# The attention front of a retention layer with two MLPs: fewer chunks ahead of the decay table, compact states, and output rests made by TensorE

## The chip, the cores and the metric

The kernel runs on one core of one Trainium2 chip. The metric is device microseconds of one execution. A core has TensorE (PE: matrix products out of SBUF into PSUM; PEld is its weight load), VectorE (DVE), ScalarE (ACT), GpSimd (POOL) and SyncE (SP). SP and ScalarE also issue DMA transfers, each on a queue of its own; 16 DMA engines carry them. Each engine works through its instructions in program order and waits on semaphores for the others.

## The reference

A retention (linear attention) layer comes first, with a decay factor `lam` for each of 8 heads, over 2 batches of 768 tokens, head size 64. Its output, 1536 tokens of 512 channels, goes through two MLPs (512 to 2048 to 512). The first has a leaky rectifier with a learned slope, the second a squared rectifier.

```python
for b in range(nb):
    intra = np.einsum('bhic,bhjc->bhij', qb, kb) * Dmask[None]     # lam ** (i - j), lower triangle
    intra = np.einsum('bhij,bhjd->bhid', intra, vb)
    inter = np.einsum('bhid,bhde->bhie', qb * lam_pow[None], kv_state)
    out[:, :, sl] = intra + inter
    kb_dec = kb * rev_pow[None]
    kv_state = lam_block[None, :, None, None] * kv_state + np.einsum('bhsd,bhse->bhde', kb_dec, vb)
...
h = x @ w_in
g = np.maximum(h, 0.0) + alpha * np.minimum(h, 0.0)     # second MLP: g = np.maximum(h, 0.0) ** 2
return (g @ w_out).astype(np.float32)
```

The weights are float64, and everything else is float32.

## The kernel before

**Precision.** A product of the MLPs is three passes over float32r operands (12 bits of mantissa): each operand is split into a float32r value `h` and the exact rest `l`, and lh, hl and hh are summed in PSUM. So whatever enters an MLP is needed twice: `xh` (a cast) and `xl = x - xh`. The attention runs in plain float32, which TensorE does in two passes per product.

**Weights.** They arrive as raw float64 bits in 64 pieces of 512 KB. Piece 2f is the f-th slice (128 hidden channels) of the first w_in, piece 2f + 1 that of w_out; pieces from 32 on are the second MLP's. `load_piece` issues a piece on ScalarE's queue, three ahead. `Conversion` turns a piece into float32r and rest: `start` (two ScalarE operations, issued one piece ahead), `begin` (three VectorE operations), `middle` (one VectorE operation, then ScalarE's cast `wh`, then the load of a further piece) and `end` (VectorE: `wl`). One such round is called a unit below. Before, pieces are converted in the order 0, 1, 2, ...

**The decay table.** VectorE computes powers of `lam` on 8 partitions into `z`, SP writes `z` to HBM (`zd`) and reads it back in two skewed forms, `dec` (the mask, 128 x 8 x 128) and `grow` (powers for the state's part). The ten loads of q and k for five chunks are issued ahead of `zd` on SP's queue, and v, r (the keys again, tokens on partitions) of chunks 0 and 1 on ScalarE's.

**Attention.** There are 12 chunks of 128 tokens: chunk index 0 to 5 with the two batches alternating, so chunk n + 2 continues chunk n's state. The eight heads go in four pairs. For each chunk:

- `scores(n)`: k^T q, eight products on two row tiles (64 x 128) into two PSUM banks. Chunks 0 to 4 (LA = 5) run ahead of the table; ScalarE copies their scores to SBUF.
- `decay(n)`: VectorE multiplies the scores by `dec`, in two halves, from SBUF for chunks 0 to 4 and out of PSUM for the others.
- `factors(n)`: GpSimd multiplies q by `grow` and r by a column of `dec`.
- `outputs(n)`: TensorE adds into one bank `po`: v and decayed scores (two column tiles), then the state times q (full 128 x 128, the state being a block diagonal of two heads with zeros beside it). `pk` is r^T v, again a full 128 x 128 product of which only the two diagonal blocks are used.
- `keep_output(n)`: ScalarE casts `po` to `xh`, VectorE subtracts for `xl`.
- `keep_state(n)`: VectorE adds the two diagonal blocks of `pk` to the decayed old state, one instruction for each; ScalarE scales the new state by lam ** 128 in four instructions, for the chunk after next.

The loop over n writes the order of each engine out by hand: loads for later chunks, `outputs(n)`, `decay(n + 4)`, a unit if `EARLY_UNITS[n]` says so (chunks 3 to 8 and 10: seven units), `keep_output(n)`, `keep_state(n)`, `factors(n + 2)`, `scores(n + 5)`. The decays of a unit chunk stand between the steps of `begin`.

**MLPs.** Then come 48 steps per MLP, each for one tile of 512 tokens and one hidden slice: `first` (12 passes into one of three banks), activation, `rest`, and, two steps later, `second` (12 passes into four of five banks). The first six steps are slices 0 to 5 of token tile 0, so each needs two new pieces of weights; one piece is converted per step.

PSUM has eight banks; before, one pool holds tags for them, and attention and MLPs take turns on them.

Of the kernel before, what the change touches and what calls it, by code (L numbers as in the profile page):

```python
# [23 lines left out]
TT = 512  # tokens of an MLP tile  # L24
# [17 lines left out]
def retention_then_two_mlps(  # L42
# [26 lines left out]
    psum = ctx.enter_context(tc.tile_pool(name="psum", bufs=1, space=PSUM))  # L69
# [4 lines left out]
    used = {}  # L74

    def bank(name, banks):
        """The next of some banks of PSUM."""
        i = used[banks] = used.get(banks, -1) + 1
        return psum.tile([128, 512], F32, tag=f"bank{banks[i % len(banks)]}", name=name)

    def pair_bank(name, banks):
        return bank(name, banks).rearrange("p (a i) -> p a i", a=NPAIR)

# [6 lines left out]
    # Piece 2 f is the slice of w_in for the f-th 128 hidden channels, piece 2 f + 1 that of w_out.  # L90
    # Piece j of 4 NF: the second pair's come behind the first's.
    wpools = {}
    raws, bits, weights = {}, {}, {}

    def load_piece(j):
        if j < 4 * NF:
            raws[j] = raw = rawp.tile([128, DM, 2], U32, tag="raw", name=f"raw{j}")
            w = (w1, w2)[j // (2 * NF)]
            nc.scalar.dma_start(raw.rearrange("p a b -> p (a b)"), w[j % (2 * NF)])

    class Conversion:
        def __init__(self):
            self.j = 0

        def start(self, j):
            if j < 4 * NF:
# [5 lines left out]
        def begin(self, between=()):  # L112
            """Exponent of 11 -> 8 bits: its top bit and its low 7. Below float32's range all are 0."""
            between = iter(between)
            if self.j == 0:
                self.start(0)
            self.start(self.j + 1)
            x, high = bits[self.j], raws[self.j][:, :, 1]
            nc.vector.tensor_scalar(x.bitcast(F32), x.bitcast(F32), LEAST, None, ALU.max)  # L119
            next(between, lambda: None)()  # L120
            nc.vector.tensor_scalar(x, x, 3, 0x3FFFFFF8, ALU.logical_shift_left, ALU.bitwise_and)  # L121
            next(between, lambda: None)()
# [4 lines left out]
        def middle(self):  # L127
            """The lower word, rounded to the last three bits."""
            j = self.j
# [4 lines left out]
            load_piece(j + AHEAD)  # L134
            weights[j] = hi

        def end(self):
            j = self.j
# [4 lines left out]
            self.j += 1  # L143
# [6 lines left out]
    # (MLP, token tile, hidden slice, slices that are summed in PSUM together)  # L150
# [64 lines left out]
    def partial_sum(m, t, f, part, i):  # L215
# [3 lines left out]
        # The same operand stays in the array where it can.  # L219
# [52 lines left out]
    z = ap1.tile([H, ZW], F32, name="z")  # L272
    nc.vector.memset(z[:, 0 : CH - 1], 0.0)
    qk_t, vk_t = {}, {}
# [8 lines left out]
    def load_vk(n):  # L283
        queue = nc.scalar if n < 2 else nc.sync
        v_t = kp.tile([128, H, D], F32, tag="v", name=f"v{n}")
        queue.dma_start(v_t, vr[n])
        r_t = None
        if ORDER[n][0] < NCH - 1:
            r_t = kp.tile([128, H, D], F32, tag="r", name=f"r{n}")
            queue.dma_start(r_t, kr[n])  # L290
# [5 lines left out]
    pw = pair_bank("warm_ps", (0, 2))  # L296
    for i in range(WARM):
        nc.tensor.matmul(pw[:, i % NPAIR, :], warm, warm, start=True, stop=True)

# [292 lines left out]
```

## Time and profile before

| | |
|---|---|
| time, median of 3 runs | 602.98 us (602.83 to 604.35) |
| span of the profiled execution | 600.4 us (the page lists no other time of this execution) |
| TensorE busy | 578.9 us, 96% |
| VectorE busy | 360.7 us, 60% |
| ScalarE busy | 298.0 us, 50% |
| GpSimd busy | 29.8 us, 5% |
| first product of the MLPs starts | 74.43 us into the span |
| DMA moved | 54.23 MB |

Busy shares are means over the span. The attention and the MLPs load the engines in quite different ways, so they are read stage by stage. The profile's times count from the first instruction of the span. `xN` behind a row is the number of instructions in it. On TensorE a float32 product counts as two matmul instructions, and the ends of matmuls are modelled, so distances between starts tell more than durations.

### The profile page before, as it was taken

The numbers are of one execution on the slowest core, as the hardware profiler recorded it, in microseconds if no ns is written. First come the engines' busy times: TensorE is split into PE (matmuls) and PEld (weight loads), VectorE is DVE, ScalarE is ACT, GpSimd is POOL, SyncE is SP. The second block draws the span as 40 slices with busy tenths as digits, with TensorE's granted clock in tenths as the row PEclk, the third lists the DMA queues.
The fourth block names the chain that finished last, engine by engine and source line by source line (L and its number), as shares of the span: only waits on it lengthen the run. The fifth ranks groups of instructions, "written<-read, shape, count | busy, mean of one in ns | idle before, by whom it ended". The sixth has DMA issues, their size and how long they took to land.

```text
span 600.4 us, 7487 instructions
## 1 busy us (share of the span) xinstructions
PE 578.9 (96%) x2868; PEld 481.8 (80%) x2868; DVE 360.7 (60%) x625; ACT 298.0 (50%) x515; POOL 29.8 (5%) x29
## 2 busy tenths in 40 slices
PE   7697699999999999999999999999999999999997
PEld 6586588888888888888888888888888888888886
DVE  3889989675777777777887797773222222222221
ACT  4254678665666676665676465542322222322222
POOL 1674000000000000000000000000000000000000
PEclk9698999999999999999999999999999999999999
DMA  8994333324422231233333232210100000100001
GB/s 285 345 301 140 106 106 128 131 94 158 157 90 88 105 106 62 79 105 106 105 109 102 72 105 96 81 36 0 72 0 1 0 1 1 70 1 0 1 1 70
DMA packets 21667, 54.23 MB, mean 90 GB/s; under 512 B 2424, under 2 KB 3968, under 8 KB 21632
## 3 DMA queue, kind: packets, MB, share of 16 engines
q10 hardware_dynamic: 9792, 34.61, 16.6%
q1 hardware_dynamic: 11840, 19.16, 9.4%
q8 instruction: 22, 0.36, 0.2%
q14 instruction: 13, 0.11, 0.1%
HBM read 48.50 MB, written 5.25 MB: 90 GB/s over the span
## 4 chain that ended last, share of the span: by engine, by line
PE 89%; DVE 6%; DMA 2%; issue 1%; ACT 1%; DVEq 0%; SPq 0%
PE h L167 43%; PE acc L225 22%; PE acc L223 22%; DMA dec<-zd 1%; DVE sc L392 1%; DVE state L449 1%; PE o L417 1%; DVE bits L131 1%; DVE wl L141 1%; DVE bits L119 1%; DVE xal L441 1%; DMA zd<-z 1%; PE pk L431 1%; DVE bits L123 0%; DVE bits L121 0%
## 5 line engine op out<-in xcount | busy, mean ns | idle before, releaser
L177 DVE SCALAR_TENSOR_TENSOR g<-h,g 128x512 f32<-128x512 f32 x48 | 33.1, 691 | 127.9 <-ACT g L176 127.9
L186 ACT CAST gh<-g 128x512 fp32r<-128x512 f32 x96 | 59.6, 621 | 85.8 <-DVE g L177 37.8
L176 ACT ACTIVATE g<-h 128x512 f32<-128x512 f32 x48 | 28.7, 597 | 133.2 <-PE h L167 133.2
L191 DVE TENSOR_TENSOR gl<-g,gh 128x512 fp32r<-128x512 f32 x96 | 66.5, 692 | 32.0 <-ACT gh L186 24.9
L167 PE MATMUL h<-xah,wl 128*128 128x512 f32 x192 | 74.8, 390 | 0.0
L167 PE MATMUL h<-xah,wh 128*128 128x512 f32 x192 | 74.7, 389 | 0.0
L223 PE MATMUL acc<-gh,wh 128*128 128x512 f32 x192 | 74.7, 389 | 0.0
L225 PE MATMUL acc<-wh,gh 128*128 128x512 f32 x192 | 74.7, 389 | 0.0
L167 PE MATMUL h<-xal,wh 128*128 128x512 f32 x192 | 74.7, 389 | 0.0
L223 PE MATMUL acc<-gl,wh 128*128 128x512 f32 x192 | 74.7, 389 | 0.0
L167 PE MATMUL h<-xbh,wl 128*128 128x512 f32 x192 | 74.7, 389 | 0.0
L225 PE MATMUL acc<-wh,gl 128*128 128x512 f32 x192 | 74.7, 389 | 0.0
L223 PE MATMUL acc<-gh,wl 128*128 128x512 f32 x192 | 74.7, 389 | 0.0
L167 PE MATMUL h<-xbl,wh 128*128 128x512 f32 x192 | 74.7, 389 | 0.0
L167 PE MATMUL h<-xbh,wh 128*128 128x512 f32 x192 | 74.7, 389 | 0.0
L225 PE MATMUL acc<-wl,gh 128*128 128x512 f32 x192 | 74.7, 389 | 0.0
L181 DVE SCALAR_TENSOR_TENSOR g<-h,g 128x512 f32<-128x512 f32 x44 | 30.4, 691 | 44.1 <-ACT g L180 44.0
L133 ACT CAST wh<-bits 128x512 fp32r<-128x512 f32 x64 | 39.8, 622 | 17.3 <-DVE bits L131 17.2
L123 DVE SCALAR_TENSOR_TENSOR bits<-raw,bits 128x512 uint32<-128x512 uint32 x64 | 44.2, 691 | 2.0
L141 DVE TENSOR_TENSOR wl<-bits,wh 128x512 fp32r<-128x512 f32 x64 | 44.5, 695 | 0.9 <-ACT wh L133 0.7
L131 DVE CUSTOM_DVE_ANT_0 bits<-raw,bits 128x1024 uint16<-128x1024 uint16 x64 | 44.7, 698 | 0.0
L109 ACT ACTIVATE bits<-raw 128x512 f32<-128x512 f32 x64 | 42.9, 671 | 0.0
(74 smaller groups left out, 833.0 us busy)
## 6 DMA issues: line engine op xcount, KB each, us to landing
raw<-in_w_dram ACTq DMA_DIRECT2D x64, 512.0 KB, 3.3
k<-in_kt_dram SPq DMA_DIRECT2D x12, 256.0 KB, 5.4
q<-in_qt_dram SPq DMA_DIRECT2D x12, 256.0 KB, 5.6
out_dram<-p SPq DMA_DIRECT2D x12, 256.0 KB, 2.3
v<-in_vr_dram SPq DMA_DIRECT2D x10, 256.0 KB, 4.9
r<-in_kr_dram SPq DMA_DIRECT2D x8, 256.0 KB, 5.2
sums<-p SPq DMA_DIRECT2D x8, 256.0 KB, 2.2
ps<-sums SPq DMA_DIRECT2D x8, 256.0 KB, 3.0
```

The costliest lines, as they stand in the source:

```text
L109: nc.scalar.activation(x.bitcast(F32), high.bitcast(F32), AF.Abs)
L123: nc.vector.scalar_tensor_tensor(x, high, 0xC0000000, x, ALU.bitwise_and, ALU.bitwise_or)
L131: nc.vector.tensor_tensor(x.bitcast(I32), x.bitcast(I32), low.bitcast(I32), ALU.add)
L133: nc.scalar.copy(hi, x.bitcast(F32))
L141: nc.vector.tensor_tensor(lo, x, hi.bitcast(F32), ALU.subtract)
L167: nc.tensor.matmul(ph, w[:, cols], x[:, c, :], start=c == 0 and i == 0, stop=c == NC - 1 and i == 2)
L177: nc.vector.scalar_tensor_tensor(g, ph, 0.0, g, ALU.max, ALU.mult)
L181: nc.vector.scalar_tensor_tensor(g, ph, 0.0, g, ALU.max, ALU.subtract)
L186: nc.scalar.copy(gh, g)
L191: nc.vector.tensor_tensor(gl, g, gh.bitcast(F32), ALU.subtract)
L223: nc.tensor.matmul(acc[t][i], w[:, cols], g, **flags)
L225: nc.tensor.matmul(acc[t][i], g[:, cols], w, **flags)
```

## The change

- Three chunks (LA = 3) run their scores ahead of the decay table instead of five, and the pools of q, k, v, r keep their number of buffers (scores have four instead of six). Raw piece 0 is loaded at the very front (ScalarE's queue) and v, r of chunk 0 stand on SP's queue between `zd` and `dec`; those of chunk 1 and q, k of chunk 3 follow `grow`.
- The tensor engine's warming products are 12 ahead of the scores and 10 behind those of chunk 2.
- Piece 0 is converted before the loop, and five more in the loop (chunks 3, 5, 6, 8, 9): six in all. Pieces are converted and loaded in the order 0, 2, 1, 4, 3, 6, 5, ... The loads of the early pieces go on SP's queue.
- Scores of a chunk are one PSUM tile of two banks; a decay is one instruction of 128 x 1024, out of SBUF for chunks 0 and 1 and out of PSUM from chunk 2 on. It is issued two chunks ahead (DA).
- A state holds only its two 64 x 64 blocks (128 x 4 x 64). Its product with q is eight products of 64 x 64, and `pk` eight of 128 x 64. VectorE's add is one instruction of 128 x 256.
- `xl` is no longer made by VectorE: TensorE adds -I times `xh` to `po` (float32r, one product of 512 columns), after the scores of a later chunk, and ScalarE copies the result to `xl`.
- Attention has PSUM pools of its own (two buffers for scores, outputs and pk each), and the MLPs' pool is opened behind them.

```diff
-LA = 5  # chunks whose scores run ahead
+LA = 3
+DA = 2
-WARM = 10  # products that only warm the tensor engine up
-EARLY_UNITS = [0, 0, 0, 1, 1, 1, 1, 1, 1, 0, 1, 0]  # whether a weight piece goes with a chunk
+WARM = 12, 10
+EARLY_UNITS = [0, 0, 0, 1, 0, 1, 1, 0, 1, 1, 0, 0]
+SEQ = [0] + [p for f in range(1, 2 * NF) for p in (2 * f, 2 * f - 1)] + [4 * NF - 1]
...
-    def load_piece(j):
-        if j < 4 * NF:
+    def load_piece(queue=nc.scalar):
+        if len(loaded) < 4 * NF:
+            j = SEQ[len(loaded)]
+            loaded.append(j)
...
-            nc.scalar.dma_start(raw.rearrange("p a b -> p (a b)"), w[j % (2 * NF)])
+            queue.dma_start(raw.rearrange("p a b -> p (a b)"), w[j % (2 * NF)])
...
-            load_piece(j + AHEAD)
+            if load:
+                load_piece(nc.sync if len(loaded) < 2 * EARLY else nc.scalar)
...
-    qp = actx.enter_context(tc.tile_pool(name="qp", bufs=LA + 2))
-    kp = actx.enter_context(tc.tile_pool(name="kp", bufs=LA))
+    qp = actx.enter_context(tc.tile_pool(name="qp", bufs=LA + 4))
+    kp = actx.enter_context(tc.tile_pool(name="kp", bufs=LA + 2))
...
+    psc = actx.enter_context(tc.tile_pool(name="psc", bufs=2, space=PSUM))
+    pso = actx.enter_context(tc.tile_pool(name="pso", bufs=2, space=PSUM))
+    psk = actx.enter_context(tc.tile_pool(name="psk", bufs=2, space=PSUM))
...
+    def keep_warm(i):
+        pw = pso.tile([128, NPAIR, CH], F32, tag="o", name=f"warm_ps{i}")
+        for a in range(WARM[i]):
+            nc.tensor.matmul(pw[:, a % NPAIR, :], warm, warm, start=True, stop=True)
+    less = ap1.tile([128, CH], F32R, name="less")
+    lessf = ap1.tile([128, CH], F32, name="lessf")
+    nc.gpsimd.affine_select(
+        lessf, warm, pattern=[[-1, CH]], compare_op=ALU.not_equal, fill=-1.0, base=0,
+        channel_multiplier=1,
+    )
+    nc.scalar.copy(less, lessf)
+    keep_warm(0)
+    load_piece()
     for n in range(LA):
         load_qk(n)
...
     nc.sync.dma_start(zd, z)
+    load_vk(0)
...
+    load_vk(1)
+    load_qk(LA)
...
-            st = ap1.tile([128, NPAIR, 128], F32, name=f"state{b}_{r}")
-            nc.gpsimd.memset(st, 0.0)
-            state[b, r] = st
+            state[b, r] = ap1.tile([128, NPAIR, D], F32, name=f"state{b}_{r}")
...
-        if n < LA:
-            for t in range(2):
-                nc.scalar.copy(sc[:, t], ps[t])
-            sc_t[n] = sc, None
-        else:
-            sc_t[n] = sc, ps
+        if n < LA - 1:
+            nc.scalar.copy(sc, ps)
+            ps = sc
+        sc_t[n] = sc, ps
...
-        nc.vector.tensor_tensor(sc[:, t], s, dec_v[:, t], ALU.mult)
+        nc.vector.tensor_tensor(sc, ps, dec_v, ALU.mult)
...
-                nc.tensor.matmul(
-                    po[:, a, :], state[b, c % 2][:, a, :], q_t[:, a, :], start=False, stop=True,
-                    skip_group_check=True,
-                )
+                for t in range(2):
+                    d = slice(t * D, (t + 1) * D)
+                    nc.tensor.matmul(
+                        po[d, a, :], state[b, c % 2][d, a, :], q_t[d, a, :], start=False,
+                        stop=True, skip_group_check=True,
+                    )
...
-                nc.tensor.matmul(
-                    pk[:, a, :], r_t[:, 2 * a : 2 * a + 2, :], v_t[:, 2 * a : 2 * a + 2, :],
-                    start=True, stop=True,
-                )
+                for t in range(2):
+                    h = 2 * a + t
+                    nc.tensor.matmul(
+                        pk[t * D : (t + 1) * D, a, :], r_t[:, h, :], v_t[:, h, :], start=a == 0,
+                        stop=True, skip_group_check=True,
+                    )
...
         nc.scalar.copy(xh[:, :, cols], po)
-        nc.vector.tensor_tensor(xl[:, :, cols], po, xh.bitcast(F32)[:, :, cols], ALU.subtract)
+    def keep_rest(n, po):
...
+        nc.tensor.matmul(po, less, xh[:, :, cols], start=False, stop=True, skip_group_check=True)
+        nc.scalar.copy(xl[:, :, cols], po)
...
     for n in range(LA):
         scores(n)
         if n == 0:
-            load_vk(0)
-            load_vk(1)
+            conv.start(0)
+    keep_warm(1)
+    conv.begin(ahead=False)
+    conv.middle(load=False)
+    conv.end()
     for n in range(2):
         factors(n)
-    for n in range(LA):
-        for t in range(2):
-            decay(n, t)
+    for n in range(DA):
+        decay(n)
     for n in range(NN):
         if n + 2 < NN:
             load_vk(n + 2)
-        for i in [LA, LA + 1] if n == 0 else [n + LA + 1]:
-            if i < NN:
-                load_qk(i)
+        if n + LA + 1 < NN:
+            load_qk(n + LA + 1)
+        if n in (1, 2, 3):
+            load_piece(nc.sync)
...
         po, pk = outputs(n)
-        late = []
-        if LA <= n + LA - 1 < NN and n > 0:
-            late = [lambda t=t: decay(n + LA - 1, t) for t in range(2)]
+        if n + DA < NN:
+            decay(n + DA)
         if EARLY_UNITS[n]:
-            conv.begin(late)
+            conv.begin()
...
         keep_output(n, po)
-        if EARLY_UNITS[n]:
-            conv.middle()
         if pk is not None:
             keep_state(n, pk)
         if EARLY_UNITS[n]:
+            conv.middle()
             conv.end()
         if n + 2 < NN:
             factors(n + 2)
         if n + LA < NN:
             scores(n + LA)
+        keep_rest(n, po)
     actx.close()
+    psum["mlp"] = ctx.enter_context(
+        tc.tile_pool(name="psum", bufs=1, space=PSUM, reuse_waits="tile")
+    )
```

## Rows read from the trace of the kernel before

**Rows 1.** Busy time of each engine by stretch: us, then busy (instructions) for each.

```profile
29.64:46.34 16.70, 16.66 (x195) 14.93 (x193) 14.52 (x25) 9.24 (x22) 12.18 (x11) 1.00 0.92 309
46.34:74.43 28.09, 19.72 (x193) 17.00 (x193) 26.86 (x48) 16.73 (x37) 6.63 (x5) 0.94 0.33 113
74.43:597.00 522.57, 522.52 (x2307) 432.48 (x2305) 302.49 (x506) 260.91 (x435) 0.00 (x0) 1.00 0.20 69
...
61.30:66.60 5.30, 3.14 (x35) 2.73 (x34) 5.22 (x11) 3.52 (x9) 0.00 (x0) 1.00 0.31 109
```

**Rows 2.** Chain of waits in order of time: start, us, what.

```profile
0.74 1.33 DMA lam_sb<-in_lam_dram
...
7.68 3.61 DMA zd<-z
11.35 6.43 DMA dec<-zd
17.88 3.05 DVE sc L392 x2
...
588.79 8.17 PE acc L225 x36
```

**Rows 3.** Timeline of TensorE, chunk 0 and chunk 2: start, us, group.

```profile
20.98 1.97 PE L417 MATMUL o<-sc,v 128*64 128x128 f32 x14 [0.78 <-DVE sc L392]
...
29.64 1.09 PE L417 MATMUL o<-sc,v 128*64 128x128 f32 x16
30.67 1.16 PE L423 MATMUL o<-q,state 128*128 128x128 f32 x8
31.66 1.06 PE L431 MATMUL pk<-v,r 128*128 128x128 f32 x8
32.65 1.16 PE L378 MATMUL s<-q,k 64*128 64x128 f32 x16
```

**Rows 4.** Waits of TensorE, 17.88 to 74.43: total, times, longest.

```profile
PE o L417 <- DVE xal L441: 4.6, 4, 1.8
```

**Rows 5.** DMA rate in the first 20 us, slices of 0.5 us.

```profile
GB/s 0 0 0 0 33 299 397 307 217 234 291 361 381 397 344 356 389 401 389 397 404 404 393 393 391 225 345 293 280 240 269 202 252 202 237 282 331 356 377 402
```

**Rows 6.** Groups by shape, first 75 us: count, busy us, mean ns, idle before.

```profile
L392 DVE TENSOR_TENSOR sc<-sc,dec 128x512 f32<-128x512 f32 x10 | 10.9, 1155 | 10.2 <-DMA dec<-zd 10.2
...
L392 DVE TENSOR_TENSOR sc<-s,dec 128x512 f32<-128x512 f32 x14 | 9.4, 682 | 0.2
...
L440 ACT CAST xah<-o 128x512 fp32r<-128x512 f32 x11 | 6.3, 572 | 10.4 <-PE o L417 9.3 <-PE o L423 1.1
```

**Rows 7.** The same for VectorE, 56 to 67 us.

```profile
L449 DVE TENSOR_TENSOR state<-pk,old 64x256 f32<-64x256 f32 x4 | 1.7, 418 | 0.0
L441 DVE TENSOR_TENSOR xal<-o,xah 128x512 fp32r<-128x512 f32 x2 | 1.4, 680 | 0.0
L123 DVE SCALAR_TENSOR_TENSOR bits<-raw,bits 128x512 uint32<-128x512 uint32 x2 | 1.4, 679 | 0.0
...
L119 DVE TENSOR_SCALAR bits<-bits 128x512 f32<-128x512 f32 x3 | 1.3, 418 | 0.0
```

**Rows 8.** The same for VectorE, 38 to 45 us.

```profile
L119 DVE TENSOR_SCALAR bits<-bits 128x512 f32<-128x512 f32 x1 | 1.3, 1276 | 0.0
```

**Rows 9.** Stretches, TensorE alone: us, busy, granted clock, DMA share, GB/s.

```profile
13.20:14.00 0.80, 0.01 (x1) 1.00 1.14 325
...
15.50:16.00 0.50, 0.00 (x0) 0.65 1.12 202
...
25.50:26.00 0.50, 0.50 (x8) 0.61 1.07 324
```

**Rows 10.** Timeline of VectorE, steps 2 and 3 of the MLPs.

```profile
90.53 0.69 DVE L141 TENSOR_TENSOR wl<-bits,wh 128x512 fp32r<-128x512 f32 x1
...
94.90 0.68 DVE L141 TENSOR_TENSOR wl<-bits,wh 128x512 fp32r<-128x512 f32 x1
```

**Rows 11.** Timeline of TensorE, first product of step 5.

```profile
96.31 0.39 PE L167 MATMUL h<-xah,wl 128*128 128x512 f32 x1
```

More of the change, by code (lines that the diff above doesn't have):

```diff
@@ L74, in retention_then_two_mlps @@
     used = {}
+    psum = {}
     def bank(name, banks):
         i = used[banks] = used.get(banks, -1) + 1
-        return psum.tile([128, 512], F32, tag=f"bank{banks[i % len(banks)]}", name=name)
-    def pair_bank(name, banks):
-        return bank(name, banks).rearrange("p (a i) -> p a i", a=NPAIR)
+        return psum["mlp"].tile([128, 512], F32, tag=f"bank{banks[i % len(banks)]}", name=name)
     def x_tile(name, i):
@@ L93, in retention_then_two_mlps, with start @@
     raws, bits, weights = {}, {}, {}
[L95 to L96 removed]
+    loaded = []
+    def load_piece(queue=nc.scalar):
+        if len(loaded) < 4 * NF:
+            j = SEQ[len(loaded)]
+            loaded.append(j)
             raws[j] = raw = rawp.tile([128, DM, 2], U32, tag="raw", name=f"raw{j}")
             w = (w1, w2)[j // (2 * NF)]
[L99 removed]
+            queue.dma_start(raw.rearrange("p a b -> p (a b)"), w[j % (2 * NF)])
     class Conversion:
         def __init__(self):
[L103 to L106 removed]
+            self.k = 0
+        def start(self, k):
+            if k < 4 * NF and SEQ[k] not in bits:
+                j = SEQ[k]
                 low, high = raws[j][:, :, 0], raws[j][:, :, 1]
@@ L110, in start, with begin @@
                 nc.scalar.activation(low.bitcast(I32), low, AF.Copy, scale=2.0**-29)
[L112 to L118, printed above, removed]
+        def begin(self, ahead=True):
+            j = SEQ[self.k]
+            self.start(self.k)
+            if ahead:
+                self.start(self.k + 1)
+            x, high = bits[j], raws[j][:, :, 1]
             nc.vector.tensor_scalar(x.bitcast(F32), x.bitcast(F32), LEAST, None, ALU.max)
-            next(between, lambda: None)()
             nc.vector.tensor_scalar(x, x, 3, 0x3FFFFFF8, ALU.logical_shift_left, ALU.bitwise_and)
-            next(between, lambda: None)()
             nc.vector.scalar_tensor_tensor(
@@ L272, in retention_then_two_mlps @@
     z = ap1.tile([H, ZW], F32, name="z")
+    ones, tens = ap1.tile([H, 8], F32, name="ones"), ap1.tile([H, 16], F32, name="tens")
+    err = ap1.tile([H, NB], F32, name="err")
     nc.vector.memset(z[:, 0 : CH - 1], 0.0)
+    nc.vector.memset(err[:, 0:1], 0.0)
+    nc.vector.memset(ones[:, 0:1], 1.0)
+    nc.vector.memset(tens[:, 0:1], 1.0)
     qk_t, vk_t = {}, {}
@@ L283, in load_vk @@
     def load_vk(n):
-        queue = nc.scalar if n < 2 else nc.sync
         v_t = kp.tile([128, H, D], F32, tag="v", name=f"v{n}")
-        queue.dma_start(v_t, vr[n])
+        nc.sync.dma_start(v_t, vr[n])
         r_t = None
@@ L329, in retention_then_two_mlps @@
     nc.vector.tensor_tensor(sq, sq, err, ALU.add)
-    ones, tens = ap1.tile([H, 8], F32, name="ones"), ap1.tile([H, 16], F32, name="tens")
-    nc.vector.memset(ones[:, 0:1], 1.0)
-    nc.vector.memset(tens[:, 0:1], 1.0)
     for b in range(4):
@@ L373, in scores @@
         q_t, k_t = qk_t[n]
-        ps = [pair_bank(f"s{t}_{n}", (t, t + 2)) for t in range(2)]
+        ps = psc.tile([128, 2, NPAIR, CH], F32, tag="s", name=f"s{n}")
         for a in range(NPAIR):
@@ L445, in keep_state @@
         new = state[b, (c + 1) % 2]
-        for t in range(2):
-            d = slice(t * D, (t + 1) * D)
-            if c > 0:
-                nc.vector.tensor_tensor(new[d, :, d], pk[d, :, d], old_t[n][d, :, d], ALU.add)
-            else:
-                nc.scalar.copy(new[d, :, d], pk[d, :, d])
+        if c > 0:
+            nc.vector.tensor_tensor(new, pk, old_t[n], ALU.add)
+        else:
+            nc.scalar.copy(new, pk)
         if c < NCH - 2:
-            old_t[n + B] = old = ap2.tile([128, NPAIR, 128], F32, tag="old", name=f"old{n}")
+            old_t[n + B] = old = ap2.tile([128, NPAIR, D], F32, tag="old", name=f"old{n}")
             for a in range(NPAIR):
@@ L515, in retention_then_two_mlps @@
             sums_end = s >= LAG and steps[s - LAG][2] == steps[s - LAG][3][-1]
-            unit = conv.j < 4 * NF and not sums_end
-            if conv.j >= 2 * NF and unit and free[(conv.j - 2 * NF) // 2] >= s:
+            unit = conv.k < 4 * NF and not sums_end
+            if unit and SEQ[conv.k] >= 2 * NF and free[(SEQ[conv.k] - 2 * NF) // 2] >= s:
                 unit = False
```

34 lines of the change are left out of this document (11 added, 23 removed).

## The prediction

> **What bounds the kernel now.** I read the table of stretches first, then the chain of waits, then single engines inside one stretch. From 74.43 us on TensorE is busy 522.52 of 522.57 us at full clock [rows 1], and this stage's matmuls end the chain [rows 2]. The change gives this stage the same products, so its length stays; what can move is its start, 74.43 us. Ahead of it lie three parts. Until 17.88 us everything waits for the decay table: zd leaves at 7.68 us and lands 3.61 us later, dec takes 6.43 us more [rows 2]. From 29.64 to 46.34 us TensorE is busy 16.66 of 16.70 us [rows 1] and sets the pace, 4.10 us a chunk, from four groups of 1.03, 0.99, 0.99 and 1.09 us (differences of their starts; the next chunk starts at 33.74) [rows 3]. From 46.34 to 74.43 us VectorE is busy 26.86 of 28.09 us and TensorE only 19.72; a chunk with a weight piece takes VectorE 5.3 us (5.22 busy) [rows 1], and TensorE's longest waits there are for xal, the rest of the output, on VectorE [rows 4].
>
> No time of the profiled execution itself is listed beside its span of 600.4 us. The median of the runs, 602.98, lies 2.6 us above it; I take that as what surrounds the span, before and after alike.
>
> **Part 1: the way to the first output.** Before, ten q and k loads (2.6 MB) stand in front of zd on SP's queue. After, six of them and one weight piece do: 2.1 MB. Transfers begin to flow at about 2.2 us and run at some 370 GB/s [rows 5], so these end at 2.2 + 5.7 = 7.9 us; z is ready at 7.6. A lone small transfer took 1.33 us (lam) [rows 2], so zd lands at about 9.4 instead of 11.29. v0 and r0 (0.52 MB, 1.4 us) now stand ahead of dec on the same queue. While dec moved, the rate sank to 200 to 290 GB/s [rows 5]: its 0.52 MB take 1.8 to 2.6 us. That gives 9.4 + 1.3 + 0.6 (what is left of v0 and r0) + 2.6 = 13.9; the other end is the old 6.43 us again, 15.8. I take 14.3, nearer the built-up sum because fewer bytes compete.
>
> decay(0) becomes one instruction of 128x1024. From SBUF, with GpSimd at work on r beside it, a half of it took 1155 ns in the mean [rows 6], and the first two halves 3.05 us [rows 2]; read from PSUM a half took 682 ns [rows 6]. So 1.2 to 3.05 us; I take 2.2, near the mean of two. TensorE then starts at 16.5 us; before, its full stream started at 20.98 [rows 3].
>
> Moved into the wait for dec, at no cost: piece 0 is converted (about 3 us of VectorE, which stands idle from 7.7 to 17.88 there); two more warming products ahead and ten behind scores 2; the small memsets; the -I matrix. The last stands ahead of raw0's issue on ScalarE's queue; its two instructions are not in the trace, and I bound them by 0 and a GpSimd product of 1.1 us each (12.18 us for eleven) [rows 1]. If dec came 3 us earlier than I think, VectorE's and ScalarE's cover would still hold; a longer warming would then cost up to 2 us. The state memsets that go lay in idle GpSimd.
>
> **Part 2: what a chunk costs TensorE.** Intra stays 1.03, scores 1.09 [rows 3]. The state's product goes from 8 passes of 128x128 to 16 of 64x64 in two diagonal tiles. No such tile is in the trace; the nearest row is the o product, 16 passes in two column tiles in 1.03 us. Side by side it stays 1.03; one tile after the other it is 2.05; half, 0.5, is the low end. I take 1.03. The pk product becomes 16 passes that move 64 columns each: 0.5 (o halved) to 1.03 (o); I take 0.8. The rest product is one pass of 512 columns, and 36 such take 8.17 us [rows 2]: 0.23. The array's shape now changes five times a chunk instead of three; in rows 3 the starts follow each other over such changes without a gap, so nothing.
> All together: intra 12 x 1.03 = 12.4; scores 9 x 1.09 = 9.8 (three chunks lie ahead of the table instead of five, so two more are inside); state 10 x 1.03 = 10.3; pk 10 x 0.8 = 8.0; rest 12 x 0.23 = 2.8. Sum 43.3 us; 35.0 with state and pk at their low ends, 55.8 with both at the high ones.
>
> **Part 3: VectorE leaves the path.** A chunk loses xal (680 ns) and one of two adds of the state (418 ns each) on VectorE [rows 7]; units go from seven to five. What TensorE lost there, 28.09 - 19.72 = 8.4 us [rows 1], is what this can give. A unit chunk keeps 1.2 (decay), 0.42 twice and 0.68 (begin), 0.42 (state) and two more of the 0.68 kind [rows 7], 4.5, and gets a new stall: wh's cast stands behind the state's four scalings on ScalarE, which I put at two instructions of the size of xh's cast (572 ns) [rows 6], 1.2 us. That is 5.7 us against TensorE's 4.2; other chunks need 1.6. Decay is issued two chunks ahead, so a unit beside a free chunk fits; units come in chunks 3, 5, 6, 8 and 9, so twice two are neighbours. Beside GpSimd it is worse: L119 took 1276 ns in one chunk there, and 418 later [rows 8, 7]. GpSimd will now be at work until the end of the loop.
> The Trainium skill ("SBUF — State Buffer", the section on the two separate sides) says that the port pair which VectorE and GpSimd share is locked for a whole instruction, not split. Rows 6, 7 and 8 agree, 1155 against 682 ns and 1276 against 418 ns; by that rule the five units would lose up to 1.6 us each, and the sum below would come out up to 5 us higher.
> What is late next is ScalarE's cast of xh, which the rest product needs; the whole next chunk stands behind that on TensorE. pk and scores, 1.9 us, cover it. In the last chunks this cover is gone: no scores from chunk 9 on, no pk in 10 and 11. Three bare turns of about 0.7: 2.0. For the late units and other interlocks I add 3.0 (0, if the lead of two holds, to 8, five units at 1.6).
>
> **Part 4: clock.** TensorE fell to 1.2 GHz between 15.5 and 16.0 us, its last group having ended near 13.2, and was back at 2.4 GHz between 25.5 and 26.0, after five us of work [rows 9]. The first two chunks took 29.64 - 20.98 = 8.66 us instead of 2 x 3.11 [rows 3]: 2.4 lost. After, the second warming ends nearer to the restart, at perhaps 12 to 14 us. Loss 0 to 2.4; I keep 2.4, as a gap of some 3 us is near the one after which it fell.
>
> **Part 5: the MLPs.** Six pieces lead instead of seven, but in order of use. VectorE's cycle in the first steps is 4.37 us [rows 10], TensorE's 5.44 (24 passes). The tightest w_in, slice 5, falls in the fourth step as before: ready at 95.6, used at 96.31 [rows 10, 11]. New is w_out 5, in the seventh step instead of the fifth: three cycles later, 95.6 + 13.1 = 108.7, needed 13 x 2.72 us after 74.43, at 109.8. 1.1 us of air, and VectorE enters the stage without its backlog, so nothing; if that air goes, about 1 us.
>
> **The sum.** 14.3 + 2.2 + 43.3 + 2.4 + 2.0 + 3.0 = 67.2 us for the first MLP product, 7.2 earlier: span 593.2, time 595.8.
>
> **Rivals.**
> *The good end:* pk 0.5, clock kept, dec 0.8 and decay 0.7 earlier, interlocks 1.5: 3.0 + 2.4 + 0.8 + 0.7 + 1.5 less, first product at 58.8, time 587.4. For it: the shorter idle gap. Against: the port's rows.
>
> *The diagonal tiles exclude each other.* Rows 3 show two column tiles at once (o, 16 passes in 1.03 us), and two row tiles only where they write different banks (scores). Two row tiles into one bank they don't show. If these wait for each other, the state's product costs 2.05, TensorE's chunk 5.2, and the sum grows by 10 x 1.02 to 77.4: 606.0, slower. It decides from 1.75 us a product on (7.2 / 10 above 1.03). The Trainium skill ("TensorEngine Tiling (Array Packing)", Gotcha 1: PSUM Pressure) says that different row tiles can't use the same PSUM bank at one time, which read strictly is this rival; here the two write disjoint partitions, and no row so far decides.
>
> *SP's queue holds.* The pieces loaded in chunks 3, 5, 6 and 8 go through SP, which stands still until VectorE frees the buffer, some 4.1 us into the chunk; behind it wait v, r, k and q, 1.57 MB with the piece. At 370 GB/s that is 4.1 + 1.3 + 4.2 = 9.6, and scores two chunks on want q at 2 x 4.2 + 2.9 = 11.3: 1.7 us of air. With VectorE late by 3.2, three such places cost 1.5 each: 71.7, time 600.3. For it: at the old pace 309 GB/s already took 92% of the DMA engines [rows 1].
>
> **How the numbers follow.** Forecast 0.52 (its own range 591.5 to 599), good end 0.20, SP's queue 0.14, diagonal tiles 0.09, anything else above 0.05. Two in ten left out: 588 to 601. A measurement can't tell less than 0.3%, 1.8 us, from no change: below 601.2 lie the forecast, the good end and most of SP's case, 0.85; between 601.2 and 604.8 the rest of that and half-sized tile costs, 0.08; above, 0.07.
>
> **What would show it.** dec landing at 13.5 to 15 us; TensorE's restart at 16 to 17, and its clock there; starts of state, pk and scores in a middle chunk 1.03 and 0.8 apart; hardly a wait of TensorE for VectorE; the first h product at 63 to 70 us and 522.6 us from there on. I am wrong if a state product takes near 2 us, if SP's loads release TensorE or GpSimd in the middle chunks, or if gaps show in the MLP's first eight steps.

## The result, and the profile after

The changed kernel takes 597.14 us (median of 4 runs, 594.48 to 598.96), the kernel before 603.45 beside it (602.83 to 604.35): ratio 0.9896, 95% interval [0.9866, 0.9927], faster by 1.0%. The forecast was 595.8 in a range of 588 to 601.

The profiled execution is the slowest of the four: 598.96 us, span 597.2. So 1.8 us lie around the span, not the 2.6 that I took. Its three stretches answer to [rows 1]; the stretches around 16 and 61 us answer to [rows 9].

The stretches of the changed kernel: start and end, length, busy time (instructions) of each engine, granted clock, DMA share, GB/s:

```profile
core 0: us, PE busy (x) PEld busy (x) DVE busy (x) ACT busy (x) POOL busy (x), PEclk, DMA share, GB/s
0.00:24.56 24.56, 18.24 (x190) 16.52 (x190) 13.89 (x47) 9.80 (x20) 7.84 (x12) 0.93 0.84 282
24.56:71.20 46.64, 39.33 (x572) 31.67 (x571) 34.49 (x44) 26.72 (x62) 18.49 (x15) 0.96 0.67 231
71.20:597.20 526.00, 522.46 (x2305) 432.25 (x2303) 300.87 (x503) 262.96 (x437) 0.00 (x0) 1.00 0.20 70
...
15.00:16.00 1.00, 0.00 (x0) 0.00 (x0) 1.00 (x1) 0.00 (x0) 0.89 (x1) 0.81 1.01 327
16.00:19.00 3.00, 2.73 (x32) 2.64 (x32) 3.00 (x3) 0.58 (x1) 1.50 (x2) 0.50 1.04 370
19.00:20.00 1.00, 0.10 (x2) 0.01 (x1) 0.34 (x1) 0.82 (x3) 1.00 (x2) 0.98 1.04 364
...
60.00:63.00 3.00, 3.00 (x27) 2.67 (x28) 3.00 (x3) 1.73 (x3) 0.98 (x1) 0.50 0.81 264
```

The MLPs take 526.0 us from their first product to the end of the span, as before (600.4 - 74.43 = 526.0). What moved is their start: 71.20 here against 74.43. With 1.8 + 526.0 us around it, the median of 597.14 corresponds to a start at 69.3; a second profile of the same kernel (e1 below, 596.66 us) has it at 68.95.

The timeline of TensorE answers to [rows 3]: start, duration, group, and in brackets the idle time ahead of it and what ended it. o<-sc,v is a chunk's first product, o<-q,state the state's:

```profile
16.27 1.98 PE L436 MATMUL o<-sc,v 128*64 128x128 f32 x16 [3.99 <-DVE sc L411]
...
20.02 1.16 PE L400 MATMUL s<-q,k 64*128 64x128 f32 x16 [0.93 <-DMA q<-in_qt_dram]
...
24.56 1.09 PE L436 MATMUL o<-sc,v 128*64 128x128 f32 x16
25.59 1.09 PE L444 MATMUL o<-q,state 64*64 64x128 f32 x16
26.61 0.69 PE L454 MATMUL pk<-v,r 128*64 128x64 f32 x16
27.22 1.16 PE L400 MATMUL s<-q,k 64*128 64x128 f32 x16
28.31 0.49 PE L469 MATMUL o<-xah,less 128*128 128x512 f32 x1
28.74 1.09 PE L436 MATMUL o<-sc,v 128*64 128x128 f32 x16
...
34.23 0.51 PE L469 MATMUL o<-xah,less 128*128 128x512 f32 x1 [1.67 <-ACT xah L463]
...
47.39 0.50 PE L469 MATMUL o<-xah,less 128*128 128x512 f32 x1 [0.53 <-ACT xah L463]
...
52.20 1.16 PE L400 MATMUL s<-q,k 64*128 64x128 f32 x16 [1.65 <-DMA q<-in_qt_dram]
...
58.47 1.16 PE L400 MATMUL s<-q,k 64*128 64x128 f32 x16 [2.01 <-DMA q<-in_qt_dram]
...
59.99 1.97 PE L436 MATMUL o<-sc,v 128*64 128x128 f32 x16
61.89 1.81 PE L444 MATMUL o<-q,state 64*64 64x128 f32 x16
...
71.20 0.40 PE L170 MATMUL h<-xah,wl 128*128 128x512 f32 x1
```

Chunk 2 starts at 24.56 us; before, at 29.64 [rows 3]. Up to there 5.1 us are gained. From there to the MLPs the changed kernel takes 46.6 us, the one before 74.43 - 29.64 = 44.8. The two stretches don't hold the same work: with three chunks ahead of the table, seven scores are left in it instead of five, 2.2 us more. My terms come to 42.0 for it (chunk 2 at 16.5 + 2.4 of clock + two chunks of 3.15 = 25.2, and 67.2 - 25.2). Undisturbed, a chunk is 28.74 - 24.56 = 4.18 us, where 4.10 stood before. The rest is waits: [rows 4] have TensorE waiting for VectorE; now it waits for q and for xh's cast, and after the longest of these it runs at half clock (the two lines at 59.99 and 61.89 against 1.09 each).

The waits of the changed kernel up to 75 us: who waited, for what, total, times, longest:

```profile
PE s L400 <- DMA q<-in_qt_dram: 5.0, 5, 2.0
...
PE o L469 <- ACT xah L463: 3.6, 4, 1.7
...
SPq L102 <- DVE bits L133: 18.6, 4, 6.5
```

SP's queue, the issues behind one such wait (start, duration). Nothing leaves between 38.9 and 44.66 us, where the piece's load stands for VectorE:

```profile
37.66 1.21 SPq L292 DMA_DIRECT2D q<-in_qt_dram  x1
44.66 0.33 SPq L102 DMA_DIRECT2D raw<-in_w_dram  x1
...
47.19 0.42 SPq L292 DMA_DIRECT2D q<-in_qt_dram  x1
...
51.74 0.42 SPq L292 DMA_DIRECT2D q<-in_qt_dram  x1
```

In the chain of waits (start, duration) these loads stand among the longest pieces ahead of the MLPs:

```profile
7.66 2.38 DMA zd<-z
...
24.32 8.15 DMA raw<-in_w_dram
...
51.74 6.63 DMA q<-in_qt_dram
```

### The profile page after: what moved, and what is told of

Same layout as the page of the kernel before. It is cut to its first block, busy times and chain, and to the rows that moved or that the text cites. A ratio compares the mean times of both kernels' runs of the same rounds, so it can differ in the third digit from the quotient of the medians.

```text
span 597.2 us, 7851 instructions
## 1 busy us (share of the span) xinstructions
PE 580.0 (97%) x3064; PEld 480.4 (80%) x3064; DVE 349.3 (58%) x593; ACT 299.5 (50%) x518; POOL 26.3 (4%) x26
## 4 chain that ended last, share of the span: by engine, by line
PE 91%; DMA 4%; DVE 2%; ACT 1%; SPq 1%; issue 0%; ACTq 0%
PE h L170 44%; PE acc L228 22%; PE acc L226 22%; DMA q<-in_qt_dram 2%; DMA raw<-in_w_dram 1%; PE o L436 1%; PE o L444 1%; PE s L400 1%; PE o L469 1%; ACT xah L463 0%; DMA zd<-z 0%; PE pk L454 0%; DVE bits L125 0%; DVE bits L124 0%; DMA lam_sb<-in_lam_dram 0%
## 5 line engine op out<-in xcount | busy, mean ns | idle before, releaser
L144 DVE TENSOR_TENSOR wl<-bits,wh 128x512 fp32r<-128x512 f32 x64 | 46.4, 725 | 6.1 <-ACT wh L135 6.1
L125 DVE SCALAR_TENSOR_TENSOR bits<-raw,bits 128x512 uint32<-128x512 uint32 x64 | 46.2, 721 | 2.2
L133 DVE CUSTOM_DVE_ANT_0 bits<-raw,bits 128x1024 uint16<-128x1024 uint16 x64 | 44.9, 702 | 0.1
L114 ACT ACTIVATE raw<-raw 128x512 int32<-128x512 uint32 x64 | 42.7, 667 | 0.0
```

The source lines that it names most:

```text
L114: nc.scalar.activation(low.bitcast(I32), low, AF.Copy, scale=2.0**-29)
L125: nc.vector.scalar_tensor_tensor(x, high, 0xC0000000, x, ALU.bitwise_and, ALU.bitwise_or)
L133: nc.vector.tensor_tensor(x.bitcast(I32), x.bitcast(I32), low.bitcast(I32), ALU.add)
L144: nc.vector.tensor_tensor(lo, x, hi.bitcast(F32), ALU.subtract)
```

## The experiments

Ratios are to the kernel before on the same chip; the jobs ran on four chips, and the changed kernel itself is beside job 1 alone (e1 to e4). So e5 to e12 are compared by their ratios and, above all, by their own traces. Times of TensorE, from each profile (us): its restart, the start of chunk 2, the first MLP product, and the stretch between these two. In the changed kernel seven chunks of 4.18, the shorter last three and two bare turns would be about 39; without the product with -I (e3, e6) it would be about 33. The kernel before and e7 have two scores (2.2 us) fewer in this last stretch.

```
kernel     median (runs)   ratio [95%]               restart  chunk 2  MLPs   between
before     602.55 (11)     1                         20.98    29.64    74.43  44.8
after      597.14 (4)      0.9896 [0.9866, 0.9927]   16.27    24.56    71.20  46.6
e1 again   596.46 (6)      0.9904 [0.9883, 0.9926]   16.72    24.87    68.95  44.1
e2         594.97 (6)      0.9892 [0.9862, 0.9921]   16.75    27.28    67.65  40.4
e3         596.22 (6)      0.9899 [0.9873, 0.9925]   16.85    23.66    66.53  42.9
e4         595.64 (6)      0.9893 [0.9874, 0.9911]   17.83    25.96    68.20  42.2
e5         601.17 (12)     0.9975 [0.9956, 0.9993]   18.66    25.88    74.72  48.8
e6         596.58 (5)      0.9898 [0.9882, 0.9914]   16.46    26.13    69.08  43.0
e7         600.29 (12)     0.9955 [0.9930, 0.9980]   23.30    32.16    74.68  42.5
e8         604.11 (12)     1.0011 [0.9993, 1.0029]   17.64    26.86    76.00  49.1
e9         598.13 (6)      0.9934 [0.9915, 0.9954]   16.11    25.71    72.34  46.6
e10        599.14 (12)     0.9960 [0.9934, 0.9986]   17.56    24.83    68.56  43.7
e11        598.95 (6)      0.9946 [0.9929, 0.9964]   17.73    25.60    71.20  45.6
e12        596.97 (4)      0.9904 [0.9887, 0.9920]   16.53    26.45    70.60  44.2
```

**e1, the changed kernel once more.**

> The changed kernel itself, unchanged, as a second reading of its spread. Its profile had the first MLP product at 71.20 us, and its four times ran from 594.5 to 599.0, where the kernel before stays within 1.5 us. Theory A (TensorE waits for single q loads that land at times which differ from run to run, and each long wait also lowers its clock): 594 to 599 again, with waits of TensorE for q of several us in the profile. Theory B (steady lag of VectorE and ScalarE): the times would lie within 1.5 us of each other.

596.46 us, 594.14 to 598.93: a spread of 4.8 us, where the kernel before spread over 1.3 on that chip (602.02 to 603.35; on the chips of e5 to e12 it spread over 2.3 to 4.0). Its waits for q sum to 3.7 us. The longest is in chunk 8, as in the first profile (2.27 and 2.01); the others differ in size and place. Two profiles fit Theory A, that the gain changes from run to run with the moment at which loads land; they don't prove it.

**e2, weight pieces on ScalarE's queue.**

```diff
-                load_piece(nc.sync if len(loaded) < 2 * EARLY else nc.scalar)
+                load_piece()
...
-            load_piece(nc.sync)
+            load_piece()
```

> All early weight pieces are loaded on ScalarE's queue again instead of SP's. Theory A (SP stands still behind a piece until VectorE frees its buffer, and q, k, v and r stand behind that): SP's waits for VectorE go, TensorE's waits for q (5.0 us in the profile) shrink below 1.5 us, first MLP product 66 to 68 us, time 592 to 595. Theory C (the bytes are simply too many for the time, so the queue does not matter): waits for q or raw of the same 5 to 8 us in sum, time 596 to 598. Theory B (lag of VectorE): within 1 us of the changed kernel.

The waits for q are gone, as expected, and the stretch between is the shortest of all, 40.4 us. But of these 3.7 us against e1 the front lost 2.4: TensorE's clock stayed low for chunks 0 and 1, which took 10.5 us (8.2 in e1). That this is the queue's doing is not shown: with the pieces on SP's queue, e9 and e12 took 9.6 and 9.9 us there. A stretch of e2, columns as above:

```profile
16.00:30.00 14.00, 12.78 (x148) 11.07 (x148) 6.28 (x5) 5.77 (x15) 9.58 (x8) 0.64 0.96 333
```

In time it can't be told from e1: the intervals overlap.

**e3, the rest back on VectorE** (no product with -I).

```diff
+        nc.vector.tensor_tensor(xl[:, :, cols], po, xh.bitcast(F32)[:, :, cols], ALU.subtract)
...
-        keep_rest(n, po)
```

> Only the rest is undone: xl is subtracted by VectorE again (12 x 0.68 us), no product with -I and no copy on ScalarE. Theory A (TensorE is the pace, VectorE has room): TensorE saves 12 x 0.43 = 5.2 us and three bare turns of 0.7, the waits for q stay, so faster by 2 to 5 us, 592 to 595. Theory B (VectorE is what the change relieved): units now take 6.4 us on VectorE, two neighbours no longer fit, TensorE waits for the decay or po; slower by 2 to 5 us, 599 to 602.

The chunk is 3.75 us (three in a row from 23.66 on), 0.43 shorter, and the time is the same, between the ranges of the two theories. In this profile TensorE reaches the missing transfer sooner and waits longer. Timeline of TensorE in e3:

```profile
34.91 1.09 PE L436 MATMUL o<-sc,v 128*64 128x128 f32 x16
42.83 2.08 PE L400 MATMUL s<-q,k 64*128 64x128 f32 x16 [5.19 <-DMA q<-in_qt_dram]
44.84 1.97 PE L436 MATMUL o<-sc,v 128*64 128x128 f32 x16
```

**e4, wh's cast ahead of the state's scalings.**

```diff
+        if EARLY_UNITS[n]:
+            conv.middle()
         if pk is not None:
             keep_state(n, pk)
         if EARLY_UNITS[n]:
-            conv.middle()
```

> In a unit chunk the conversion's fourth step and the cast of wh stand ahead of the state's add and scalings, as in the kernel before; nothing else changes. Theory B (VectorE waits 6.1 us for the cast behind four scalings, and everything behind it is late): VectorE's wait for wh falls below 2 us, SP's wait for the buffer ends some 1 us earlier, time 1 to 3 us less. Theory A or C: VectorE's lag costs little by itself, within 1 us; the state comes 1.3 us later, but is needed two chunks on.

VectorE's wait for wh fell from 6.1 us in all to 2.4, and the time stayed within 1 us of e1: that stall seems to have stood beside other waits.

**e5, e2 with a longer second warming**, to have e2's loop and the clock too.

```diff
-WARM = 12, 10
+WARM = 12, 26
```

> The pieces on ScalarE's queue as in the run before, and the second warming is 26 products instead of 10, so that TensorE is busy until about 16.3 us, when the first decay ends. Theory D (what is left above the pace is mostly the clock: in the last run it was 0.64 of full between 16 and 30 us, and the first two chunks took 10.5 us where 6.0 would do): the clock stays at full through the restart, chunk 2 starts at 23 to 23.5 us instead of 24.6 to 27.3, the first MLP product at 63.5 to 65.5, time 590.5 to 592.5, and the spread shrinks. Rival (the clock follows something else, or the warming overruns the table): chunk 2 at 25 or later, 594 to 596.

Theory D fell. The clock held (1.00 from 16 to 30 us) and chunks 0 and 1 took 7.2 us instead of 10.5. But dec landed late, so that decay(0) started at 17.39 us and TensorE at 18.66 (the longer warming had ended at 16.1). And then ScalarE stood still for 4.31 us, ahead of its issue of a further weight piece and of the start of the next unit, with xh's cast behind them; the profile puts the end of this wait down to loads that landed. TensorE waited 4.03 for that cast, and then the clock fell after all. ScalarE in e5, then TensorE:

```profile
34.68 0.34 ACTq L102 DMA_DIRECT2D raw<-in_w_dram  x1
35.06 0.67 ACT L113 ACTIVATE bits<-raw 128x512 f32<-128x512 f32 x1 [4.31 <-DMA q<-in_qt_dram]
```

```profile
...
37.91 0.79 PE L469 MATMUL o<-xah,less 128*128 128x512 f32 x1 [4.03 <-ACT xah L463]
38.63 1.98 PE L436 MATMUL o<-sc,v 128*64 128x128 f32 x16
```

**e6, e2 and e3 together.**

> The pieces on ScalarE's queue, and the rest subtracted by VectorE again. Theory A' (with the queue free the pace is TensorE's; the product with -I costs it 0.43 us a chunk and three bare turns, and VectorE has room for 0.68 a chunk): a middle chunk falls from 4.18 to 3.75 us, first MLP product 3 to 5 us earlier than with the pieces on ScalarE alone, time 590 to 592. Theory B (VectorE, beside GpSimd, is the limit as soon as the transfers are not): TensorE waits for xal and decays, time 595 to 599.

Neither the queue nor the product with -I is left, and now VectorE is late, as Theory B has it. TensorE's waits in e6:

```profile
PE o L436 <- DVE xal L464: 5.2, 3, 3.4
...
PE s L400 <- DVE sc L411: 2.7, 2, 1.6
```

Five chunks of 3.75 us, then 7.9 us of waits for VectorE: again the same time.

**e7, scores five chunks ahead.**

```diff
-LA = 3
-DA = 2
+LA = 5
+DA = 4
...
-    qp = actx.enter_context(tc.tile_pool(name="qp", bufs=LA + 4))
-    kp = actx.enter_context(tc.tile_pool(name="kp", bufs=LA + 2))
+    qp = actx.enter_context(tc.tile_pool(name="qp", bufs=7))
+    kp = actx.enter_context(tc.tile_pool(name="kp", bufs=5))
```

> The changed kernel with five chunks ahead of the table instead of three, and the buffers and decay lead of before (four copied scores, decay issued four ahead); all else stays. Theory E (the gain lies in the front: chunk 2 came at 24.6 us instead of 29.6, and from there to the MLPs it takes as long as before): zd and dec land 2.5 to 3.5 us later, chunk 2 starts 2 to 3 us later, but two scores fewer (2.2 us) remain in the loop and q is always early; time 595 to 598, near the changed kernel. Rival (the loop gains by its lead, and q's lateness is what three chunks cost): q waits vanish and the time falls to 592 to 594.

The loop has no wait for q and takes 42.5 us, 1.6 less than e1's 44.1. But it holds two scores fewer, 2.2 us, and its waits for xh sum to 5.3 us, so no gain of the lead itself is shown. And the front lost 7 us: TensorE waited 5.6 us for ScalarE's copy of early scores, which stood behind the start of piece 0, and 2.8 for decay. Since that start moved as well, e7 doesn't price five chunks alone.

**e8, states of 128x128 as before**, and their products, two adds and memsets.

```diff
-                for t in range(2):
-                    d = slice(t * D, (t + 1) * D)
-                    nc.tensor.matmul(
-                        po[d, a, :], state[b, c % 2][d, a, :], q_t[d, a, :], start=False,
-                        stop=True, skip_group_check=True,
-                    )
+                nc.tensor.matmul(
+                    po[:, a, :], state[b, c % 2][:, a, :], q_t[:, a, :], start=False, stop=True,
+                    skip_group_check=True,
+                )
...
```

> Only the compact states are undone: 128x128 products for state and pk, two adds of 64x256, memsets on GpSimd. By the traces TensorE's pk goes from 0.61 to 0.99 us and the state's product stays (1.02 against 0.99), VectorE pays 0.43 us more a chunk for eight chunks. Theory A (waits for transfers hide a few tenths of TensorE): 0 to 2 us more, 596 to 599. Theory B (VectorE's relief is what counts): 3 to 4 us more, 599 to 601.

The whole gain is gone, more than either theory allowed; e6, on the same chip, has 0.9898, so the chip alone doesn't explain it. Its chunk is 4.53 us (26.86 to 31.39), 0.35 more over ten chunks. Chunk 2 starts 2 us later than in e1, and longer waits for q and xh come on top, up to the MLPs' door; that VectorE's second add causes them is not shown by itself. Timeline of TensorE in e8:

```profile
31.39 1.09 PE L437 MATMUL o<-sc,v 128*64 128x128 f32 x16
...
70.03 0.79 PE L466 MATMUL o<-xah,less 128*128 128x512 f32 x1 [2.20 <-ACT xah L460]
```

**e9, pieces and units later.**

```diff
-EARLY_UNITS = [0, 0, 0, 1, 0, 1, 1, 0, 1, 1, 0, 0]
+EARLY_UNITS = [0, 0, 0, 0, 0, 1, 1, 0, 1, 1, 1, 0]
...
-        if n in (1, 2, 3):
+        if n in (3, 4, 5):
```

> Only the time of the conversions moves: loads of pieces in chunks 3, 4 and 5 instead of 1, 2 and 3, units in chunks 5, 6, 8, 9 and 10 instead of 3, 5, 6, 8 and 9, everything on SP's queue as in the changed kernel. Theory C (from 10 to some 36 us the DMA engines are full; a chunk needs 1.05 MB, 2.8 us, and pieces in that time make what stands last in the queue late, a piece ahead of xh or a q ahead of scores): no wait of TensorE above 0.6 us up to chunk 5, chunk 5 starts at 37 to 38 us instead of 38.0 to 38.9, first MLP product 65 to 68, time 591 to 594. Theory A (SP's stand behind a piece, whenever it is): the same waits two chunks later, 595 to 598.

From chunk 2 to chunk 7 there is no wait at all (4.18 us each), as Theory C has it up to chunk 5; then the waits of the other kernels come, only later, and the clock with them. Timeline of TensorE in e9:

```profile
...
46.63 1.09 PE L436 MATMUL o<-sc,v 128*64 128x128 f32 x16
50.45 1.16 PE L400 MATMUL s<-q,k 64*128 64x128 f32 x16 [1.09 <-DMA q<-in_qt_dram]
...
61.45 0.79 PE L469 MATMUL o<-xah,less 128*128 128x512 f32 x1 [2.53 <-ACT xah L463]
62.18 1.98 PE L436 MATMUL o<-sc,v 128*64 128x128 f32 x16
```

**e10, xh's cast ahead of the unit's start.**

```diff
+        keep_output(n, po)
         if EARLY_UNITS[n]:
             conv.begin()
-        keep_output(n, po)
```

> Only ScalarE's order changes: the cast of xh stands ahead of the two operations that start the next piece, so xh no longer waits for a raw piece to land, nor for those 1.2 us. Theory F (in-order ScalarE hands the lateness of a piece on to TensorE by way of xh): the rest product's waits in chunks 3 to 9 (1.7 + 0.5 us in the changed kernel's profile, 4.0 and 2.0 in the one with the longer warming) go, time 1 to 3 us less, 593.5 to 595.5. Rival (the piece's lateness only moves on to the scalings and the next xh, and q stays late): within 1 us of 596.5.

One wait for xh of 1.66 us is left beside the bare turns (in the changed kernel 1.67 + 0.53), and q makes 3.0 in two places: moving one cast shifts the wait. This profile is the fastest of the twelve runs (596.28 against a median of 599.14), so it doesn't show what makes the others longer.

**e11, e9 and e10 with all pieces on ScalarE's queue.**

> Later units, xh ahead of the start of a piece, and the pieces on ScalarE's queue, together. If theories A, C and F each hold a part, nothing but the pace is left: 16.7 + 2.4 of clock + 43.6 + 2 gives a first MLP product at 64 to 66 us, time 590 to 592, and a spread below 3 us. If the transfers only change places again: 594 to 597.

No wait for q in the loop; waits for xh of 6.5 us in five places, 2.4 the longest. My expectation of a loop at its bare pace fell.

**e12, less data.**

```diff
+        if n < 4:
             k_t = kp.tile([128, NPAIR, CH], F32, tag="k", name=f"k{n}")
             nc.sync.dma_start(k_t, kt[n])
+            first_k.append(k_t)
+        else:
+            k_t = first_k[n % 4]
...
```

> The changed kernel, but k and v of chunks 4 to 11 are not loaded: these chunks use the tiles of chunks 0 to 3 again, so what they compute is not the reference's. Every engine does the same instructions; 16 transfers of 256 KB go, 0.52 of 1.05 MB a chunk from chunk 4 on. In the profiles so far chunk 2 starts at 24 to 27 us, and from there to the MLPs it takes 40 to 49 us where TensorE's products and the three bare turns need 39. Theory T (late transfers are what takes that time: a q ahead of scores, a piece ahead of xh, and the clock falls in these waits): TensorE's waits for q go, from chunk 2 to the MLPs takes 39 to 41.5 us, time 590.5 to 593.5, spread below 3 us. Rival L (lag of VectorE beside GpSimd and of ScalarE's order): TensorE's waits for xh and decays stay or take the place of those for q, 43 to 47 us, time 595 to 599. If the clock falls without a wait for transfers, it is neither.

With the DMA engines a third busy after 30 us, no wait for q is left behind 19.76 us. The four runs spread over 1.7 us (596.6 to 598.29), which fits Theory T but doesn't show it: e6, with all its transfers, spread over 2.0. The median stays. The lag now is VectorE's and ScalarE's own. Timeline of VectorE in e12, one unit beside GpSimd and then the same instructions alone:

```profile
39.84 1.30 DVE L123 TENSOR_SCALAR bits<-bits 128x512 f32<-128x512 f32 x1
...
44.27 1.42 DVE L133 CUSTOM_DVE_ANT_0 bits<-raw,bits 128x1024 uint16<-128x1024 uint16 x1
...
48.12 0.42 DVE L123 TENSOR_SCALAR bits<-bits 128x512 f32<-128x512 f32 x1
...
49.98 0.68 DVE L133 CUSTOM_DVE_ANT_0 bits<-raw,bits 128x1024 uint16<-128x1024 uint16 x1
```

ScalarE in e12 waits for that VectorE, casts wh, and xh's cast of the next chunk comes late (start, duration, idle ahead):

```profile
44.45 1.06 ACT L491 ACTIVATE old<-state,grow 128x64 f32<-128x64 f32 x4 [2.68 <-DVE state L485]
45.73 0.62 ACT L135 CAST wh<-bits 128x512 fp32r<-128x512 f32 x1 [0.22 <-DVE bits L133]
...
47.85 0.57 ACT L472 CAST xah<-o 128x512 fp32r<-128x512 f32 x1
```

Theory T, that the transfers are the loss, fell for the median and stays open for the spread; its rival, that another lag takes their place, held.

## Why the prediction was right, and where it was not

The forecast 16.5 + 43.3 + 2.4 + 2.0 + 3.0 = 67.2 stands against the profiled run's 16.3 + 43.5 + 2.8 + 1.4 + 6.8 = 70.8, close to its 71.20: restart, TensorE's work, clock, bare turns, other waits. The 0.4 that is missing lies in gaps of about 0.1 us each. That is the slowest of the four runs; for the median the start is at 69.3, 2.1 us behind the forecast, and the time missed by only 1.3 because 1.8 us lie around the span and not 2.6. That part is luck.

**Part 1 held.** zd landed at 7.66 + 2.38 = 10.04 us (forecast 9.4; the 370 GB/s of the forecast were high, [rows 5] have 344 in the mean from 2.5 to 10 us), and dec about 14.9 (14.3): decay(0), which waits for it, started at 14.99. decay(0) took less than forecast, 1.22 for 2.2. VectorE began first and GpSimd's r, 0.12 us behind it, took 2.02 us there against 1.06 later; decay(1), behind both, took 2.08. TensorE restarted at 16.27 (16.5): two misses that nearly cancel. VectorE's two decays, start and duration of both:

```profile
14.99 3.22 DVE L411 TENSOR_TENSOR sc<-sc,dec 128x1024 f32<-128x1024 f32 x2 [0.61 <-DMA dec<-zd]
```

and GpSimd's products beside them:

```profile
15.11 2.02 POOL L421 TENSOR_TENSOR r<-r,dec 128x512 f32<-128x512 f32 x1 [13.80 <-DMA dec<-zd]
18.62 1.06 POOL L421 TENSOR_TENSOR r<-r,dec 128x512 f32<-128x512 f32 x1 [1.50 <-DMA r<-in_kr_dram]
```

Two warming products more, the -I matrix (0.29 us of GpSimd, 0.30 of ScalarE) and piece 0 lay in the wait, as costed. That the gain sits here is read from where the chunks start; no run undid the front alone.

**Part 2 held in the sum, by two errors that cancel, which is luck.** The state's product costs 1.02 us (25.59 to 26.61), as long as the 16 passes of o: its diagonal tiles run side by side, and that rival fell. The strict reading of the Trainium skill ("TensorEngine Tiling (Array Packing)", Gotcha 1: PSUM Pressure), that row tiles can't use one bank at a time, is not what this trace shows, where they write different partitions. pk cost 0.61 and not 0.8, the rest product 0.43 and not 0.23: 10 x 0.19 less, 12 x 0.2 more. In all 12 x 1.02 + 9 x 1.09 + 10 x 1.02 + 10 x 0.61 + 12 x 0.43 = 43.5.
What this part overlooked: the chunk didn't get shorter, 4.18 against 4.10. e3 and e8 split it: compact states take 0.35 off TensorE, the product with -I puts 0.43 on. Without the compact states the stretch to the MLPs takes 49.1 us and the gain is gone (e8). The -I buys VectorE 0.68 us a chunk; e6, where TensorE waits 7.9 us for VectorE, suggests that this is wanted once the transfers are out of the way, and in e3 undoing it changes the time by less than can be told.

**Part 3 failed in size; this is the term that was wrong.** "For the late units and other interlocks I add 3.0": 6.8 were measured in the profiled run, q 0.93 + 1.65 + 2.01 and xh 1.67 + 0.53, and 4.2 in e1's (q 3.7, xh 0.5). TensorE waits no more for VectorE in the loop, as forecast, and most of the up to 8.4 us that this could give went to what was late next. First SP's queue, by the rival's mechanism: SP stood 18.6 us for VectorE in four places, with v, r, k and q behind. A sign that the prediction had set for being wrong came true with it: SP's loads released TensorE (q) and GpSimd (r, nine waits, 19.2 us). Then ScalarE, where xh's cast stands behind a piece that has not landed. Behind both, VectorE beside GpSimd: SP's issues wait for VectorE to free a buffer. By the Trainium skill ("SBUF — State Buffer", the two separate sides) the shared port is locked for a whole instruction. The trace fits, in decay(0) and r above, and in what GpSimd's work costs VectorE: from 24.56 to 71.20 us the unit's five instructions take 1197 ns (wl), 996 (L125), 934 (L133), 576 (L124) and 555 (L123) in the mean, where 691, 690, 680, 430 and 418 are their times alone; that sums to 1.35 us a unit, near the 1.6 set for it. By that rule the sum was up to 72, nearer to this run than mine, and not to the median's 69.3. SP's rival had 600.3; the median of 597.14 lies between it and the forecast, nearer to the forecast.
The experiments suggest, each by one profile, that these lags stand in parallel. With the pieces off SP's queue (e2) the wait for q goes, and that profile has lost clock in the front; with the clock held (e5) ScalarE stands still and xh is late; without the -I product q is waited for longer (e3); with later units the waits come later (e9); with less data VectorE and ScalarE are late (e12).

**Part 4** had the first drop, at twice its price: 1.2 us were lost where 2.4 were forecast (chunk 0's o and pk took 1.76 and 1.07 us instead of 1.02 and 0.61; the clock fell between 15 and 16 us and was back by 20). It missed the second drop: at 60 us, after a wait of 2.01, o and the state's product took 1.90 and 1.77 us instead of 1.02 each, 1.6 lost.

**Part 5 held.** 526.0 us, and TensorE busy 522.46 of it: w_out 5 was in time.

Open: what part of the higher ratios of e5, e7 and e9 to e11 is the kernels' and what the chips': none had the changed kernel beside it, and their profiled runs lie up to 2.9 us from their medians. For e5 and e7 the chip alone is no reason, as e6 on it has 0.9898. The times of e3, e5, e7, e8, e10 and e11 lie outside the ranges of both theories that I had set against each other, and that of e9 by 0.1 us, so no account here forecasts what a change of the loop is worth. No version is clearly faster than the changed kernel: e2 has the lowest median, 594.97, inside its interval.

## What to carry to other kernels

Where several engines are near their limits at once (before, VectorE 26.86 of 28.09 us in one stretch, TensorE 16.66 of 16.70 and the DMA engines 92% in the one ahead of it [rows 1]), taking work off one is worth what the next one leaves, not what was taken: work out the second and the third lag ahead of the sum. Microseconds taken from the start, where one chain of small transfers holds everything, seem to have arrived at the end: chunk 2 came 5.1 us earlier, and the median's first MLP product as much. Before comparing two stretches, count the work in each: here two scores had moved from one into the other. An engine that issues DMAs in order should not get an issue that waits for a late buffer ahead of loads that are needed sooner: in e2, without such issues on SP, the waits for q were gone, though the time can't be told from the changed kernel's. The wait of TensorE of 2.01 us was followed by half clock, 1.6 us more.

## What the runs showed of the hardware

- Two 64x64 tiles on the array's diagonal, into different partitions of one bank, run side by side: 16 passes of 128 columns in 1.02 us, where 8 passes of 128x128 took 0.99 before [rows 3]. In pk's two column tiles, 16 passes of 64 columns took 0.61.
- One float32r product of 512 columns among float32 products costs 0.43 us of the stream; in a row of its kind 0.23 (8.17 / 36) [rows 2].
- Where a decay of VectorE reads from SBUF and GpSimd works on r, the first to start kept its pace: decay(0) took 1.22 us, r, begun 0.12 us later, 2.02, and decay(1) 2.08. The decay out of PSUM at 18.13 us took 1.21 and r beside it 1.06: neither was slowed.
- dec's landing varied: decay(0), which waits for it, started between 14.83 us (e9) and 17.39 (e5) in kernels that issue the same loads ahead of it. These profiles are from several chips.
